# Output rows in transfers of 64 instead of 32, the last ones shared anew among three queues

## The chip, the cores and the metric

The kernel runs on one core of a Trainium2 chip. That core has TensorE (PE, matrix products into PSUM), VectorE (DVE), ScalarE (ACT), GpSimd (POOL) and the sync engine (SP), which only issues. DMA transfers are issued by SP, ScalarE and GpSimd, each on a queue of its own, and carried by 16 DMA engines that all queues use. The metric is the device time of one execution in microseconds (us).

## The reference

Two layers, one behind the other, with B = 8 batches, H = 8 heads, S = 576 time steps, D = 64, and H x D = 512 channels.

```python
kv  = einsum('bhsd,bhse->bhde', k, v)
o   = einsum('bhsd,bhde->bhse', q, kv)
x   = o / sqrt(mean(o*o, axis=-1) + 1e-6) * g_norm    # heads side by side: (8, 576, 512)
proj = x @ w_proj                                     # (8, 576, 1536): x1, x2, x3
conv = irfft(rfft(x2, axis=1) * rfft(filter, axis=0)) # circular, over time
out  = (x1 * conv * x3) @ w_out                       # (8, 576, 512) float32
```

The output is 8 x 576 rows of 512 float32 numbers, 2048 bytes a row and 9.44 MB in all.

## The kernel before

Everything is computed with the channels on the partitions and time along the free dimension, up to the last product, which turns this round: it takes 128 time steps as the output's partitions and 512 channels as its free dimension. The time steps lie on chip in a permuted order, in blocks of 32: one block holds steps that are 6 apart in time (`t_of`, line 156). So 32 neighbouring partitions of an output tile are 32 rows of the result that lie 6 x 2048 bytes apart.

The order of the work is written out by hand. `ORDER` (line 20) is a list of steps, `name.batch`, and the last loop (line 871) calls them one after the other; each engine and each queue executes its instructions in the order in which they were issued. The schedule interleaves up to four batches: loads (`Lk`, `Lv`, `Lq`: on the GpSimd queue, float32 in HBM, bf16 on chip, `load` at line 161), `K` (k times v), `Qt` (a DMA transpose of q on the sync queue, line 433), `O` (q times kv), the norm, the gates `Ga`/`Gb`, the forward transform `F`, products with the filter's transform `M`, the inverse `I`, `u`/`w`/`fin`, and the output product.

The output is made by these steps:

- `U0.b` and `U2.b`: each two products of 128 rows for batch b into one pair of PSUM banks. `ot0.b` and `ot2.b` copy them with ScalarE into a tile `ot` of 128 x 2 x 512 float32 (line 822) and issue its transfers through `o_dma` (line 789).
- `U4.b` for odd b: the 64 rows left over of batch b-1 and the 64 left over of batch b, as one product of 128 rows; `ot4` copies it (line 835).
- `V0.7` to `V3.7`: the last 512 rows of batch 7 (its U0 and U2 are replaced by these four). The copies `vv`, `va` (line 859; V3 is copied in two halves of the columns, one by VectorE and one by ScalarE) and each transfer have steps of their own; `ds`, `dg`, `da` issue on SP, GpSimd, ScalarE, and `da31` is column block 3, piece 1 of a tile, on ScalarE.

The tiles of `ot` come from three buffers in turn for the first 15 uses; the last five use the space of tiles that are no longer needed (`sq`, `o`, `rstd`, `x` of batch 6 and `x2`; line 806). A buffer is written again when its transfers have landed.

`out_qs` (line 796) chooses the queues: SP for the batches 0 to 5; for 6 and 7 SP and GpSimd in turn, and for their `ot4` ScalarE too. In all, 144 transfers of 32 rows (64 KB): 124 on SP, 14 on GpSimd, 6 on ScalarE.

One more transfer matters for the prediction: line 260 loads the 64 numbers of `g_norm` twice, side by side, into `g_row`, with a source pattern of [[0, 1], [0, 2], [1, 64]] (step and count of each dimension, the outermost first).

Of the kernel before, what the change touches and what calls it, by code (L numbers as in the profile page):

```python
# [19 lines left out]
ORDER = """Lf.0 Zi.0 Z.0 W.3.2 Zt.0 An.0 W.0.12 Act.0 Zg.0 Gc.0 W.1.3 Zd.0 Zf.0 Tb1.0 Lvb.0 Lkb.0 Zz.0 Ff2.0 Ff1.0 Tb0.0 Lqb.0  # L20
Ff0.0 Kb.0 eKb.0 T1.0 eTv1.0 Tb2.0 Lqa.0 T0.0 eTv0.0 O23.0 Lka.0 W.2.2 sq2.0 ov2.0 Lva.0 sq3.0 ov3.0 R3.0 rs3.0 R2.0
Lv.1 Ka.0 Lk.1 eKa.0 Lq.1 rs2.0 x1.0 Zc.0 H0.0 O01.0 sq1.0 sq0.0 ov1.0 H1.0 Lw1.0 ov0.0 R1.0 rs1.0 H2.0 W.4.2 K.1 eK.1
T1.1 eTa1.1 R0.0 rs0.0 x0.0 Lw3.0 fd0.0 HN1.0 fa0.0 HN0.0 T0.1 O23.1 sq3.1 ob3.1 eTa0.1 Ga1.0 fd1.0 Ga0.0 sq2.1 ob2.1
Lw2.0 x11.0 x10.0 O01.1 sq0.1 fa1.0 ob0.1 fr0.0 Gb0.0 g0.0 Gb1.0 Lq.2 g1.0 Ga2.0 fr1.0 sq1.1 ob1.1 x12.0 R0.1 rs0.1
Lk.2 abT.0 eT.0 R3.1 R2.1 rs3.1 rs2.1 x1.1 Lv.2 rrM.0 rrT.0 R1.1 rs1.1 err.0 abM.0 eab.0 T0.2 F0.0 Lk.3 eTs0.2 x0.1
fd.1 fr.1 T1.2 eTs1.2 Ga3.0 x13.0 K.2 eK.2 M0.0 Gb3.0 g3.0 F2.0 O01.2 sq0.2 ob0.2 Lv.3 sq1.2 F2t.0 M2.0 Gb2.0 g2.0
F1.0 F1t.0 ob1.2 O23.2 sq2.2 ob2.2 M1.0 Av1.0 rrM.1 rrT.1 err.1 Ga1.1 x11.1 Gb1.1 Ga3.1 Lk.4 sq3.2 F0.1 ob3.2 g1.1
x13.1 R2.2 rs2.2 R0.2 rs0.2 fa.1 abT.1 eT.1 Gb3.1 A0.0 M0.1 R1.2 g3.1 R3.2 rs3.2 x1.2 rs1.2 x0.2 fd.2 Lv.4 K.4 eK.4
Lq.3 abM.1 eab.1 I23.0 es23.0 K.3 eK.3 Io01.0 Ga0.1 fr.2 os01.0 Gb0.1 x10.1 Io23.0 I01.0 Ga2.1 Lq.4 os23.0 fa.2 A0.1
es01.0 g0.1 x12.1 F2.1 F2t.1 M2.1 Qt.3 O23.3 Gb2.1 g2.1 sq2.3 ob2.3 sq3.3 ob3.3 Qt.4 Ga0.2 x10.2 F1.1 O01.3 sq0.3  # L30
ob0.3 F1t.1 u.0 sq1.3 ob1.3 M1.1 abM.2 eab.2 Ga1.2 x11.2 R0.3 rs0.3 rrM.2 w.0 Av1.1 R1.3 rs1.3 rrT.2 R3.3 err.2 Qh.3
Gb1.2 rs3.3 R2.3 rs2.3 Lk.6 fin.0 g1.2 Lv.5 abT.2 eT.2 I01.1 es01.1 Io01.1 os01.1 x1.3 x0.3 fd.3 Ga3.2 x13.2 O23.4
sq3.4 ob3.4 fa.3 Gb0.2 g0.2 Gb3.2 sq2.4 ob2.4 F0.2 g3.2 Lk.5 I23.1 es23.1 Io23.1 os23.1 Ga2.2 F1.2 F1t.2 x12.2 M0.2
O01.4 abM.3 sq0.4 ob0.4 Qh.4 M1.2 sq1.4 ob1.4 F2.2 eab.3 F2t.2 Lwo.0 Lv.6 Lq.6 M2.2 Gb2.2 g2.2 Lq.5 R0.4 rs0.4 R2.4
rs2.4 Qt.5 K.5 R1.4 rs1.4 U0.0 A0.2 Av1.2 Io23.2 eK.5 ot0.0 u.1 os23.2 abT.3 eT.3 w.1 R3.4 Io01.2 os01.2 I01.2 es01.2
Ga0.3 x10.3 K.6 Gb0.3 fr.3 rrM.3 rs3.4 rrT.3 eK.6 Ga1.3 err.3 F1.3 fin.1 g0.3 Qt.6 x11.3 F1t.3 x0.4 O01.5 sq0.5 ob0.5
sq1.5 ob1.5 x1.4 fd.4 M1.3 U2.0 ot2.0 Gb1.3 fa.4 I23.2 g1.3 fr.4 es23.2 Ga2.3 x12.3 O23.5 sq3.5 sq2.5 ob2.5 ob3.5 F0.3
M0.3 U0.1 ot0.1 Ga3.3 x13.3 F2.3 A0.3 F2t.3 R0.5 R1.5 rs1.5 M2.3 Gb3.3 g3.3 R3.5 rs3.5 Gb2.3 rs0.5 g2.3 x0.5 R2.5
rs2.5 x1.5 abT.4 eT.4 Av1.3 Lv.7 O01.6 sq0.6 sq1.6 fd.5 ob0.6 ob1.6 Lk.7 U4.1 ot4.1 abM.4 u.2 eab.4 R1.6 rs1.6 Io23.3
rrM.4 rrT.4 os23.3 err.4 I01.3 es01.3 fr.5 Ga1.4 x11.4 Lq.7 I23.3 Io01.3 os01.3 Ga0.4 es23.3 x10.4 Gb0.4 w.2 fin.2  # L40
Qh.5 g0.4 R0.6 rs0.6 Ga2.4 x12.4 O23.6 sq3.6 ob3.6 Qt.7 u.3 sq2.6 ob2.6 F0.4 M0.4 rrM.5 rrT.5 err.5 Gb1.4 g1.4 F1.4
F2.4 F2t.4 M2.4 F1t.4 R3.6 rs3.6 A0.4 Gb2.4 R2.6 g2.4 Ga3.4 x13.4 rs2.6 Ga0.5 x10.5 K.7 eK.7 M1.4 Av1.4 U2.2 ot2.2
fa.5 I23.4 es23.4 Qh.6 Gb3.4 g3.4 x0.6 Io01.4 os01.4 x1.6 fr.6 abT.5 eT.5 O01.7 sq1.7 ob1.7 w.3 U2.1 sq0.7 ot2.1 ob0.7
Ga1.5 x11.5 fd.6 I01.4 es01.4 abM.5 eab.5 R0.7 rs0.7 fin.3 Io23.4 os23.4 fa.6 Gb1.5 F0.5 g1.5 M0.5 A0.5 F2.5 F2t.5
M2.5 rrM.6 rrT.6 err.6 U0.2 ot0.2 Gb0.5 F1.5 g0.5 O23.7 sq2.7 sq3.7 F1t.5 Qh.7 ob3.7 M1.5 U2.3 ob2.7 ot2.3 Ga3.5 x13.5
R2.7 rs2.7 Av1.5 u.4 w.4 fin.4 R3.7 U4.3 ot4.3 rs3.7 Gb3.5 I01.5 es01.5 I23.5 es23.5 Ga1.6 Io23.5 os23.5 g3.5 abM.6
eab.6 x11.6 F0.6 Ga2.5 abT.6 x12.5 M0.6 F1.6 Gb2.5 eT.6 Io01.5 g2.5 os01.5 F2.6 F2t.6 M2.6 F1t.6 M1.6 U0.3 Av1.6 ot0.3
u.5 U0.4 ot0.4 R1.7 rs1.7 x0.7 Ga0.6 x10.6 A0.6 Io01.6 os01.6 I01.6 es01.6 Gb1.6 g1.6 Io23.6 os23.6 I23.6 es23.6 U2.4
Gb0.6 x1.7 GaP.7 fd.7 fr.7 rrM.7 ot2.4 fa.7 rrT.7 err.7 abM.7 x1P.7 eab.7 abT.7 g0.6 F0.7 F1.7 w.5 eT.7 F2.7 F2t.7
fin.5 F1t.7 M0.7 A0.7 M2.7 U0.5 ot0.5 M1.7 U2.5 Ga2.6 ot2.5 Av1.7 u.6 Gb2.6 Gb3.6 Ga3.6 x12.6 g2.6 J01.7 x13.6 g3.6  # L50
Jo01.7 os01.7 w.6 fin.6 J23.7 Jo23.7 os23.7 es23.7 u23.7 Ga1.7 x11.7 es01.7 u01.7 Gb0.7 Ga0.7 x10.7 U0.6 ot0.6 Gb1.7
U2.6 g1.7 g0.7 fu01.7 ot2.6 GbP.7 U4.5 ot4.5 gP.7 fin23P.7 U4.7 ot4.7 V0.7 vv0.7 da02.7 ds00.7 dg01.7 GaQ.7 x1Q.7
ds03.7 GbQ.7 gQ.7 fin23Q.7 V1.7 va1.7 da12.7 ds10.7 dg13.7 dg11.7 V2.7 vv2.7 ds23.7 da22.7 dg21.7 V3.7 vv3q.7 va3p.7
ds20.7 ds30.7 da31.7 ds32.7 da33.7"""


@with_exitstack
def kernel(
# [332 lines left out]
    for n_, (d_, s_) in dict(Lw1=(wp[:, :, 0:DM], moe_w_proj[:, 0:DM]), Lw2=(wp[:, :, DM:2 * DM], moe_w_proj[:, DM:2 * DM]),  # L391
                             Lw3=(wp[:, :, 2 * DM:D3], moe_w_proj[:, 2 * DM:D3]), Lwo=(wo, moe_w_out)).items():
# [393 lines left out]
    step["u"] = lambda b: inv_u(b, 0, NDC)  # L786


    def o_dma(b, blk, t, qs, pieces=range(4)):
        for i in pieces:  # L790
            g, r = blk + i // 2, i % 2
            row = b * S + SB * (g // 3) + 2 * (g % 3) + r
            qs[i % len(qs)].dma_start(out=bass.AP(tensor=out.tensor, offset=out.offset + row * DM, ap=[[6 * DM, 32], [1, DM]]),
                                      in_=t[32 * i:32 * i + 32])
# [25 lines left out]
    def U_ev(b, c0):  # L820
        ot = ot_tile(b, c0)
        act.copy(out=ot, in_=tmp['u', b, c0])  # L822
# [10 lines left out]
    def U4_ev(b):  # L833
        ot = ot_tile(b, 4)
        act.copy(out=ot[:, 0], in_=tmp['u4', b])
        free(("u4", b))
        o_dma(b - 1, 8, ot[:, 0], out_qs(b, 4))
# [10 lines left out]
    def V(b, c):  # L848
        for h in range(1 if c < 3 else 2):
            n = DM if c < 3 else DM // 2  # L850
            t = take(("v", c, h), 1 + (c + h) % 2)
            tmp['v', c, h] = t[:, 0] if (c + h) % 2 else t
            for dc in range(NDC):
                mm2(tmp['v', c, h][:, 0:n], ygt(b)[:, dc, 64 + c * P:64 + (c + 1) * P], wo[:, dc, h * n:(h + 1) * n],
                                 start=(dc == 0), stop=(dc == NDC - 1))

    def V_ev(b, c, h, ev):
        n = DM if c < 3 else DM // 2
        ev(out=ot_tile(b, c // 2 * 2)[:, c % 2, h * n:(h + 1) * n], in_=tmp['v', c, h][:, 0:n])
# [47 lines left out]
```

## Time and profile before

| | |
|---|---|
| median of 3 runs | 214.08 us (214.07 to 215.18) |
| the profiled execution | 215.22 us, its span 213.4 us, mean TensorE clock 0.987 |
| TensorE busy | 201.6 us, 94% of the span |
| ScalarE, VectorE, GpSimd busy | 154.8, 174.8, 58.6 us |
| bytes moved by DMA | 29.61 MB; HBM read 33.69 MB, written 9.44 MB |
| output transfers on SP from `ot` | 108 of 64 KB, 1.7 us from issue to landing (median) |

The span runs from the first to the last instruction of the profiled execution; its time is measured around it. Issues of transfers appear in the profile under the queue that issues them (SPq, ACTq, or POOL), with the time that the issue took; the time to landing is from the start of the issue to the last completion. Packets are the single pieces that the DMA engines move; each transfer adds small packets of 4 bytes that report its completion.

### The profile page before, as it was taken

To read this page: it belongs to the slowest core of one execution; us is meant where nothing else is said; L and a number is where in the kernel's file an instruction comes from. 1 tells how busy PE (TensorE), PEld (TensorE's weight loads), DVE (VectorE), ACT (ScalarE), POOL (GpSimd) and SP (SyncE) were. 2 spreads that over 40 slices of the span, in tenths; PEclk is the share of its full clock that TensorE was granted. 3 is DMA by queue.
4 is the path that set the end of the run, shared out by engine and by line. 5 is a ranking of instruction groups with operands and counts; after the bars stand their busy time and mean duration, and the time that the engine had idled before them with its cause. 6 is when DMAs were issued, how large, how long until landed. Compare 5 with 4: busy or idle time off the path is not lost.

```text
span 213.4 us, 5926 instructions
## 1 busy us (share of the span) xinstructions
PE 201.6 (94%) x2472; PEld 135.3 (63%) x2472; DVE 174.8 (82%) x242; ACT 154.8 (73%) x249; POOL 58.6 (27%) x86
## 2 busy tenths in 40 slices
PE   7998779999998999999999999999999999999991
PEld 5564447576786677677665868675575574476550
DVE  6565887599893999999979999899896999997631
ACT  3787786999787998897989985794866565345430
POOL 7970391027007800400053004002201200400642
PEclk9999988999999999999999999999999999999997
DMA  4999999999999999955749944151450254051475
GB/s 64 181 203 202 205 178 200 204 197 158 197 141 182 158 205 204 196 97 117 154 114 138 235 81 96 28 136 40 98 136 16 49 139 109 20 142 41 118 214 160
DMA packets 39966, 29.61 MB, mean 139 GB/s; under 512 B 14500, under 2 KB 35556, under 8 KB 39940
## 3 DMA queue, kind: packets, MB, share of 16 engines
q0 software_dynamic: 22016, 17.76, 54.0%
q1 hardware_dynamic: 17636, 11.08, 23.1%
q10 hardware_dynamic: 288, 0.39, 0.6%
q8 instruction: 19, 0.31, 0.6%
q14 instruction: 7, 0.06, 0.1%
HBM read 33.69 MB, written 9.44 MB: 202 GB/s over the span
## 4 chain that ended last, share of the span: by engine, by line
PE 72%; DMA 12%; DVE 5%; POOL 4%; ACT 2%; issue 2%; POOLq 0%; DVEq 0%; ACTq 0%
PE ps L112 32%; PE ps L115 32%; DMA vb<-in_v_dram 9%; DMA qT<-qb 3%; PE ps L485 2%; PE ps L408 2%; PE ps L574 1%; POOL Y L652 1%; DVE tpw L646 1%; PE ps L638 1%; ACT rstd L512 1%; PE ps L612 1%; DVE x L526 1%; DVE HM L380 1%; PE ps L632 1%
## 5 line engine op out<-in xcount | busy, mean ns | idle before, releaser
L652 POOL TENSOR_TENSOR Y<-tpw 97x1024 bf16<-97x1024 f32 x8 | 18.9, 2360 | 108.9 <-DVE tpw L646 69.7
L112 PE MATMUL ps<-x,wp 128*128 128x288 bf16 (+2 forms) x264 | 37.8, 295 | 0.9 <-DVE x L526 0.7
L646 DVE TENSOR_TENSOR tpw<-ps,HH 97x2048 f32<-97x2048 f32 (+1 forms) x16 | 36.6, 2288 | 1.7 <-PE ps L112 0.9
L115 PE MATMUL ps<-x,wp 128*64 128x288 bf16 x496 | 34.6, 286 | 0.0
L112 PEld LDWEIGHTS <-wp 128*128 128x128 bf16 x264 | 26.0, 100 | 10.7 <-issue 1.9
L679 DVE TENSOR_TENSOR g<-ps,x 128x576 bf16<-128x576 f32 x30 | 22.5, 756 | 10.7 <-PE ps L112 5.3
L115 PEld LDWEIGHTS <-wp 128*64 128x64 bf16 x496 | 28.0, 110 | 3.5 <-issue 0.7
L591 ACT CAST x<-ps 128x1024 bf16<-128x1024 f32 (+1 forms) x24 | 21.0, 879 | 8.4 <-PE ps L574 5.6
L512 ACT ACTIVATE rstd<-ps,bias_eps 128x576 bf16<-128x576 f32 x32 | 23.0, 748 | 5.3 <-PE ps L115 2.5
L677 ACT CAST x<-ps 128x576 bf16<-128x576 f32 x30 | 19.6, 652 | 7.9 <-PE ps L112 4.6
L112 PE MATMUL ps<-wo,yg 128*128 128x512 bf16 (+1 forms) x104 | 23.6, 372 | 0.2 <-DVE yg L767 0.2
L739 ACT CAST eo<-ps 128x576 bf16<-128x576 f32 x32 | 19.9, 659 | 5.1 <-PE ps L112 3.8
L501 ACT ACTIVATE sq<-ps 128x576 bf16<-128x576 f32 x32 | 20.4, 653 | 3.1 <-PE ps L485 3.1
L508 ACT ACTIVATE o<-ps,g_col 128x576 bf16<-128x576 f32 x28 | 20.6, 748 | 0.0
L822 ACT COPY ot<-ps 128x1024 f32<-128x1024 f32 x12 | 12.2, 1016 | 8.9 <-PE ps L112 7.6
L115 PE MATMUL ps<-wp,ab 128*64 128x512 bf16 x144 | 17.5, 380 | 0.0
L112 PEld LDWEIGHTS <-yg 128*128 128x128 bf16 x104 | 9.6, 98 | 11.6 <-issue 1.4
L526 DVE TENSOR_TENSOR x<-o,rstd 128x1152 bf16<-128x1152 bf16 x16 | 11.6, 753 | 4.8 <-ACT rstd L512 4.8
L115 PEld LDWEIGHTS <-ind 128*64 128x64 bf16 x130 | 9.8, 121 | 7.2 <-DVE HH L380 1.8
L661 DVE TENSOR_TENSOR Y<-ps,HM 128x1024 bf16<-128x1024 f32 x8 | 9.8, 1223 | 3.2 <-PE ps L638 3.1
L115 PEld LDWEIGHTS <-ab 128*64 128x64 bf16 x144 | 7.9, 110 | 5.9 <-issue 0.3
L115 PE MATMUL ps<-wo,yg 128*64 128x512 bf16 x88 | 10.6, 380 | 0.0
(159 smaller groups left out, 347.0 us busy)
## 6 DMA issues: line engine op xcount, KB each, us to landing
out_dram<-ot SPq DMA_DIRECT2D x108, 64.0 KB, 1.7
vb<-in_v_dram POOLq DMA_DIRECT2D x7, 576.0 KB, 11.3
kb<-in_k_dram POOLq DMA_DIRECT2D x7, 576.0 KB, 11.1
qb<-in_q_dram POOLq DMA_DIRECT2D x7, 576.0 KB, 13.2
wp<-in_moe_w_proj_dram POOLq DMA_DIRECT2D x3, 512.0 KB, 15.2
fn<-in_moe_filter_fft_dram POOLq DMA_DIRECT2D x1, 576.0 KB, 6.5
vb<-in_v_dram POOLq DMA_DIRECT2D x2, 288.0 KB, 7.3
kb<-in_k_dram POOLq DMA_DIRECT2D x2, 288.0 KB, 6.8
```

The source lines that it names most:

```text
L112: nc.tensor.matmul(out, lhsT, rhs, start=start, stop=stop)
L115: nc.tensor.matmul(out[c:min(c + 64, m)], lhsT[:, c:min(c + 64, m)], rhs, start=start, stop=stop, tile_position=(0, c))
L501: act.activation(out=halves(sq()[:, j]), in_=tmp['o', b, j][:, :, 0:TH], func=AF.Square)
L508: act.activation(out=by_time(osb(), j), in_=i_, func=AF.Copy, scale=g_col)
L512: act.activation(out=by_time(rstd(), j), in_=by_row(tmp['r', b, j]), func=AF.Abs_reciprocal_sqrt, scale=1.0 / D, bias=bias_eps)
L526: vec.tensor_mul(out=xt(b)[:, j0:j1], in0=osb()[:, j0:j1], in1=rstd()[:, j0:j1])
L591: act.copy(out=o_(), in_=tmp[key, b])
L646: vec.tensor_mul(out=t_[:n], in0=xp[:n].unsqueeze(1).to_broadcast([n, 2, 2, DM]), in1=two)
L652: op(out=Yt()[:n, 2 * g:2 * g + 2], in0=t_[:n, ::-1, 0], in1=t_[:n, ::-1, 1])
L677: act.copy(out=x1, in_=pp[:, :, 0:TH])
L679: vec.tensor_mul(out=halves(g13t(b)[:, dc]), in0=pp[:, :, 0:TH], in1=x1)
L739: act.copy(out=eo()[:, h, d0:d0 + 2], in_=tmp['i', b, d0, h][:, :, 0:TH])
```

## The change

`o_dma` issues two transfers per tile of 128 rows in place of four. Each takes 64 neighbouring partitions, which are two blocks of 32: the DRAM side has a new outermost dimension of 2 with a step of one row (the two row phases of a group), and inside it the 32 rows that are 6 rows apart. `out_qs` no longer gives ScalarE a share of `ot4.7`. The transfers of V0 to V3 are 8 in place of 16, on SP (4), GpSimd (2) and ScalarE (2). In all there are 72 transfers of 128 KB: 63 on SP, 7 on GpSimd, 2 on ScalarE. `ORDER` is broken into lines elsewhere; beside this only its last steps differ.

```diff
...
-Jo01.7 ... V0.7 vv0.7 da02.7 ds00.7 dg01.7 GaQ.7 x1Q.7
-ds03.7 GbQ.7 gQ.7 fin23Q.7 V1.7 va1.7 da12.7 ds10.7 dg13.7 dg11.7 V2.7 vv2.7 ds23.7 da22.7 dg21.7 V3.7 vv3q.7 va3p.7
-ds20.7 ds30.7 da31.7 ds32.7 da33.7"""
+Jo01.7 ... V0.7
+vv0.7 ds00.7 dg01.7 GaQ.7 x1Q.7 GbQ.7 gQ.7 fin23Q.7 V1.7 va1.7 ds10.7 da11.7 V2.7 vv2.7 dg20.7 ds21.7
+V3.7 vv3q.7 va3p.7 da30.7 ds31.7"""
...
-    def o_dma(b, blk, t, qs, pieces=range(4)):
+    def o_dma(b, blk, t, qs, pieces=range(2)):
         for i in pieces:
-            g, r = blk + i // 2, i % 2
-            row = b * S + SB * (g // 3) + 2 * (g % 3) + r
-            qs[i % len(qs)].dma_start(out=bass.AP(tensor=out.tensor, offset=out.offset + row * DM, ap=[[6 * DM, 32], [1, DM]]),
-                                      in_=t[32 * i:32 * i + 32])
+            g = blk + i
+            row = b * S + SB * (g // 3) + 2 * (g % 3)
+            qs[i % len(qs)].dma_start(out=bass.AP(tensor=out.tensor, offset=out.offset + row * DM, ap=[[DM, 2], [6 * DM, 32], [1, DM]]),
+                                      in_=t[64 * i:64 * i + 64])
 
     def out_qs(b, c):
-        if b < B - 2:
-            return (nc.sync,)
-        return (nc.sync, nc.gpsimd) if c < 4 else (nc.sync, nc.gpsimd, nc.scalar, nc.gpsimd)
+        return (nc.sync,) if b < B - 2 else (nc.sync, nc.gpsimd)
...
-        for i in range(4):
+        for i in range(2):
             for e, q_ in (("s", nc.sync), ("g", nc.gpsimd), ("a", nc.scalar)):
                 step["d%s%d%d" % (e, c, i)] = lambda b, c=c, i=i, q_=q_: o_dma(b, 1 + 2 * c, ot_tile(b, c // 2 * 2)[:, c % 2], (q_,), (i,))
```

More of the change, by code (lines that the diff above doesn't have):

```diff
@@ L17 @@
 MAGIC = 3.0 * (2.0 ** 22)
[L20 to L52, printed above, removed]
-ds03.7 GbQ.7 gQ.7 fin23Q.7 V1.7 va1.7 da12.7 ds10.7 dg13.7 dg11.7 V2.7 vv2.7 ds23.7 da22.7 dg21.7 V3.7 vv3q.7 va3p.7
@@ L54 @@
-ds20.7 ds30.7 da31.7 ds32.7 da33.7"""
+ORDER = """Lf.0 Zi.0 Z.0 W.3.2 Zt.0 An.0 W.0.12 Act.0 Zg.0 Gc.0 W.1.3 Zd.0 Zf.0 Tb1.0 Lvb.0 Lkb.0
+Zz.0 Ff2.0 Ff1.0 Tb0.0 Lqb.0 Ff0.0 Kb.0 eKb.0 T1.0 eTv1.0 Tb2.0 Lqa.0 T0.0 eTv0.0 O23.0 Lka.0
+W.2.2 sq2.0 ov2.0 Lva.0 sq3.0 ov3.0 R3.0 rs3.0 R2.0 Lv.1 Ka.0 Lk.1 eKa.0 Lq.1 rs2.0 x1.0
+Zc.0 H0.0 O01.0 sq1.0 sq0.0 ov1.0 H1.0 Lw1.0 ov0.0 R1.0 rs1.0 H2.0 W.4.2 K.1 eK.1 T1.1
+eTa1.1 R0.0 rs0.0 x0.0 Lw3.0 fd0.0 HN1.0 fa0.0 HN0.0 T0.1 O23.1 sq3.1 ob3.1 eTa0.1 Ga1.0 fd1.0
@@ new lines @@
+Ga0.0 sq2.1 ob2.1 Lw2.0 x11.0 x10.0 O01.1 sq0.1 fa1.0 ob0.1 fr0.0 Gb0.0 g0.0 Gb1.0 Lq.2 g1.0
+Ga2.0 fr1.0 sq1.1 ob1.1 x12.0 R0.1 rs0.1 Lk.2 abT.0 eT.0 R3.1 R2.1 rs3.1 rs2.1 x1.1 Lv.2
+rrM.0 rrT.0 R1.1 rs1.1 err.0 abM.0 eab.0 T0.2 F0.0 Lk.3 eTs0.2 x0.1 fd.1 fr.1 T1.2 eTs1.2
+Ga3.0 x13.0 K.2 eK.2 M0.0 Gb3.0 g3.0 F2.0 O01.2 sq0.2 ob0.2 Lv.3 sq1.2 F2t.0 M2.0 Gb2.0
+g2.0 F1.0 F1t.0 ob1.2 O23.2 sq2.2 ob2.2 M1.0 Av1.0 rrM.1 rrT.1 err.1 Ga1.1 x11.1 Gb1.1 Ga3.1
+Lk.4 sq3.2 F0.1 ob3.2 g1.1 x13.1 R2.2 rs2.2 R0.2 rs0.2 fa.1 abT.1 eT.1 Gb3.1 A0.0 M0.1
@@ new lines @@
+R1.2 g3.1 R3.2 rs3.2 x1.2 rs1.2 x0.2 fd.2 Lv.4 K.4 eK.4 Lq.3 abM.1 eab.1 I23.0 es23.0
+K.3 eK.3 Io01.0 Ga0.1 fr.2 os01.0 Gb0.1 x10.1 Io23.0 I01.0 Ga2.1 Lq.4 os23.0 fa.2 A0.1 es01.0
+g0.1 x12.1 F2.1 F2t.1 M2.1 Qt.3 O23.3 Gb2.1 g2.1 sq2.3 ob2.3 sq3.3 ob3.3 Qt.4 Ga0.2 x10.2
+F1.1 O01.3 sq0.3 ob0.3 F1t.1 u.0 sq1.3 ob1.3 M1.1 abM.2 eab.2 Ga1.2 x11.2 R0.3 rs0.3 rrM.2
+w.0 Av1.1 R1.3 rs1.3 rrT.2 R3.3 err.2 Qh.3 Gb1.2 rs3.3 R2.3 rs2.3 Lk.6 fin.0 g1.2 Lv.5
+abT.2 eT.2 I01.1 es01.1 Io01.1 os01.1 x1.3 x0.3 fd.3 Ga3.2 x13.2 O23.4 sq3.4 ob3.4 fa.3 Gb0.2
@@ new lines @@
+g0.2 Gb3.2 sq2.4 ob2.4 F0.2 g3.2 Lk.5 I23.1 es23.1 Io23.1 os23.1 Ga2.2 F1.2 F1t.2 x12.2 M0.2
+O01.4 abM.3 sq0.4 ob0.4 Qh.4 M1.2 sq1.4 ob1.4 F2.2 eab.3 F2t.2 Lwo.0 Lv.6 Lq.6 M2.2 Gb2.2
+g2.2 Lq.5 R0.4 rs0.4 R2.4 rs2.4 Qt.5 K.5 R1.4 rs1.4 U0.0 A0.2 Av1.2 Io23.2 eK.5 ot0.0
+u.1 os23.2 abT.3 eT.3 w.1 R3.4 Io01.2 os01.2 I01.2 es01.2 Ga0.3 x10.3 K.6 Gb0.3 fr.3 rrM.3
+rs3.4 rrT.3 eK.6 Ga1.3 err.3 F1.3 fin.1 g0.3 Qt.6 x11.3 F1t.3 x0.4 O01.5 sq0.5 ob0.5 sq1.5
+ob1.5 x1.4 fd.4 M1.3 U2.0 ot2.0 Gb1.3 fa.4 I23.2 g1.3 fr.4 es23.2 Ga2.3 x12.3 O23.5 sq3.5
@@ new lines @@
+sq2.5 ob2.5 ob3.5 F0.3 M0.3 U0.1 ot0.1 Ga3.3 x13.3 F2.3 A0.3 F2t.3 R0.5 R1.5 rs1.5 M2.3
+Gb3.3 g3.3 R3.5 rs3.5 Gb2.3 rs0.5 g2.3 x0.5 R2.5 rs2.5 x1.5 abT.4 eT.4 Av1.3 Lv.7 O01.6
+sq0.6 sq1.6 fd.5 ob0.6 ob1.6 Lk.7 U4.1 ot4.1 abM.4 u.2 eab.4 R1.6 rs1.6 Io23.3 rrM.4 rrT.4
+os23.3 err.4 I01.3 es01.3 fr.5 Ga1.4 x11.4 Lq.7 I23.3 Io01.3 os01.3 Ga0.4 es23.3 x10.4 Gb0.4 w.2
+fin.2 Qh.5 g0.4 R0.6 rs0.6 Ga2.4 x12.4 O23.6 sq3.6 ob3.6 Qt.7 u.3 sq2.6 ob2.6 F0.4 M0.4
+rrM.5 rrT.5 err.5 Gb1.4 g1.4 F1.4 F2.4 F2t.4 M2.4 F1t.4 R3.6 rs3.6 A0.4 Gb2.4 R2.6 g2.4
@@ new lines @@
+Ga3.4 x13.4 rs2.6 Ga0.5 x10.5 K.7 eK.7 M1.4 Av1.4 U2.2 ot2.2 fa.5 I23.4 es23.4 Qh.6 Gb3.4
+g3.4 x0.6 Io01.4 os01.4 x1.6 fr.6 abT.5 eT.5 O01.7 sq1.7 ob1.7 w.3 U2.1 sq0.7 ot2.1 ob0.7
+Ga1.5 x11.5 fd.6 I01.4 es01.4 abM.5 eab.5 R0.7 rs0.7 fin.3 Io23.4 os23.4 fa.6 Gb1.5 F0.5 g1.5
+M0.5 A0.5 F2.5 F2t.5 M2.5 rrM.6 rrT.6 err.6 U0.2 ot0.2 Gb0.5 F1.5 g0.5 O23.7 sq2.7 sq3.7
+F1t.5 Qh.7 ob3.7 M1.5 U2.3 ob2.7 ot2.3 Ga3.5 x13.5 R2.7 rs2.7 Av1.5 u.4 w.4 fin.4 R3.7
+U4.3 ot4.3 rs3.7 Gb3.5 I01.5 es01.5 I23.5 es23.5 Ga1.6 Io23.5 os23.5 g3.5 abM.6 eab.6 x11.6 F0.6
@@ new lines @@
+Ga2.5 abT.6 x12.5 M0.6 F1.6 Gb2.5 eT.6 Io01.5 g2.5 os01.5 F2.6 F2t.6 M2.6 F1t.6 M1.6 U0.3
+Av1.6 ot0.3 u.5 U0.4 ot0.4 R1.7 rs1.7 x0.7 Ga0.6 x10.6 A0.6 Io01.6 os01.6 I01.6 es01.6 Gb1.6
+g1.6 Io23.6 os23.6 I23.6 es23.6 U2.4 Gb0.6 x1.7 GaP.7 fd.7 fr.7 rrM.7 ot2.4 fa.7 rrT.7 err.7
+abM.7 x1P.7 eab.7 abT.7 g0.6 F0.7 F1.7 w.5 eT.7 F2.7 F2t.7 fin.5 F1t.7 M0.7 A0.7 M2.7
+U0.5 ot0.5 M1.7 U2.5 Ga2.6 ot2.5 Av1.7 u.6 Gb2.6 Gb3.6 Ga3.6 x12.6 g2.6 J01.7 x13.6 g3.6
+Jo01.7 os01.7 w.6 fin.6 J23.7 Jo23.7 os23.7 es23.7 u23.7 Ga1.7 x11.7 es01.7 u01.7 Gb0.7 Ga0.7 x10.7
@@ L57 @@
+U0.6 ot0.6 Gb1.7 U2.6 g1.7 g0.7 fu01.7 ot2.6 GbP.7 U4.5 ot4.5 gP.7 fin23P.7 U4.7 ot4.7 V0.7
+vv0.7 ds00.7 dg01.7 GaQ.7 x1Q.7 GbQ.7 gQ.7 fin23Q.7 V1.7 va1.7 ds10.7 da11.7 V2.7 vv2.7 dg20.7 ds21.7
+V3.7 vv3q.7 va3p.7 da30.7 ds31.7"""
 @with_exitstack
```

## The prediction

> **What bounds the kernel now.** I read the engine table and the chain of waits first, then the issues and queues of the DMA engines, because the change touches nothing but output transfers.
>
> ```profile
> PE 201.6 (94%) x2472; PEld 135.3 (63%) x2472; DVE 174.8 (82%) x242; ACT 154.8 (73%) x249; POOL 58.6 (27%) x86
> ...
> PE 72%; DMA 12%; DVE 5%; POOL 4%; ACT 2%; issue 2%; POOLq 0%; DVEq 0%; ACTq 0%
> ```
>
> TensorE bounds it: 94% of the span, 72% of the chain that ended last. Output transfers appear in that chain only in its last microseconds. The second place to look is the sync queue's own timeline (start, duration, queue, line, operation, count), because it gives the moments at which output appears:
>
> ```profile
> 95.97 4.78 SPq L793 DMA_DIRECT2D out_dram<-ot  x8
> 100.91 2.88 SPq L433 DMA_TRANSPOSE qT<-qb  x1
> 104.62 14.34 SPq L793 DMA_DIRECT2D out_dram<-ot  x20
> 126.27 2.92 SPq L433 DMA_TRANSPOSE qT<-qb  x1
> 135.97 56.74 SPq L793 DMA_DIRECT2D out_dram<-ot  x76
> 198.58 1.72 SPq L793 DMA_DIRECT2D out_dram<-sq  x4
> 201.29 1.82 SPq L793 DMA_DIRECT2D out_dram<-o  x4
> ```
>
> Nothing leaves before 95.97 us. The rest of the sync queue's share is 4 transfers from `ot` (the program's U4.5), 1 from `rstd` and 7 from `x` after 203 us. Third, the queues and the issues, which tell how one transfer is spread over the 16 DMA engines:
>
> ```profile
> DMA packets 39966, 29.61 MB, mean 139 GB/s; under 512 B 14500, under 2 KB 35556, under 8 KB 39940
> ## 3 DMA queue, kind: packets, MB, share of 16 engines
> q0 software_dynamic: 22016, 17.76, 54.0%
> q1 hardware_dynamic: 17636, 11.08, 23.1%
> q10 hardware_dynamic: 288, 0.39, 0.6%
> ...
> HBM read 33.69 MB, written 9.44 MB: 202 GB/s over the span
> ```
>
> ```profile
> out_dram<-ot SPq DMA_DIRECT2D x108, 64.0 KB, 1.7
> ...
> out_dram<-x SPq DMA_DIRECT2D x7, 64.0 KB, 1.8
> out_dram<-x ACTq DMA_DIRECT2D x5, 64.0 KB, 1.8
> ...
> qT<-qb SPq DMA_TRANSPOSE x5, 4.9
> out_dram<-rstd ACTq DMA_DIRECT2D x1, 64.0 KB, 2.2
> ...
> g_row<-in_g_norm_dram SPq DMA_DIRECT2D x1, 0.5 KB
> ```
>
> **How a transfer is shared out.** Queue 10 is ScalarE's: 5 + 1 transfers of 32 rows are 192 packets of 2 KB, and it counts 288, so each transfer adds 16 small packets: one completion for each of 16 engines. Its access pattern has 32 as outermost count on both sides. Now the sync queue, whose 17636 packets hold one transfer of another kind. Its 124 output transfers make 124 x 48 = 5952. The 11684 left are five transposes and the load of `g_row`. A transpose of 576 KB in pieces of 256 B (the size of the packets recorded at that queue beside the 2 KB rows) is 2304, and with 32 completions 2336; five make 11680. That leaves 4 for `g_row`: two pieces of 256 B and two completions. Line 260 describes `g_row` with an outermost count of 2 (behind a count of 1), and it ran on two engines. So the rows show 16 shares where the outermost count is 32 and two where it is 2.
>
> The changed `o_dma` describes the DRAM side as [[DM, 2], [6*DM, 32], [1, DM]]: the outermost count is 2, not 32; the SBUF side counts 64 partitions. If the outermost count decides, 128 KB go through two engines and fourteen stand idle. That is the step on which the forecast rests, and it is inferred from one small transfer.
>
> The Trainium skill, "DMA: Bandwidth & Descriptors", on why a DMA increments its semaphore by 16, states it as a rule: the number of engines is the largest up to 16 that divides the size of the slowest dimension, other than 1, on both sides. The packets of `g_row` agree with it. The same section says that the sync and scalar queues then take the lowest-numbered engines; no view here names an engine.
>
> **The change part by part.** *Transfers.* 144 transfers of 32 rows become 72 of 64. By the code, batches 0 to 5 issue all on the sync queue, the two last share: sync 63 (4 + 10 + 38 + 2 + 2 + 2 + 1 + 4 in the order of the timeline above), ScalarE 2, GpSimd 7.
>
> *Price of a row on an engine.* What an engine can carry is read where the DMA engines are full, in the windows (PE, PEld, DVE, ACT, POOL, clock, DMA share, GB/s):
>
> ```profile
> 20.00:40.00 20.00, 17.06 (x226) 11.17 (x226) 14.33 (x28) 16.04 (x27) 7.54 (x8) 0.91 1.26 196
> ...
> 150.00:160.00 10.00, 10.00 (x83) 6.38 (x80) 9.57 (x10) 7.54 (x12) 0.79 (x2) 1.00 0.49 122
> ```
>
> The loads of 20 to 40 us are counted in the bf16 that they write (q0's 17.76 MB, 0.92 MB of it output, against 33.69 MB read from HBM), so 196 GB/s written are 392 GB/s read, 24.5 GB/s for each engine. A row of 2048 B then takes 84 ns. The other end is queue 10: 0.6% of 16 x 213.4 us is 20.5 us for 192 rows, 107 ns with all that two rows on one engine cost each other. (From 150 to 160 us, 122 GB/s at a share of 0.49 give 132 ns, but there two packets overlap on an engine and both are counted.) I take 84 ns, since two engines with a standing backlog are full as in the load stretch; the single packets of queue 10 mostly took 84, and none under 81.
>
> *Price of the output.* A transfer of 64 rows on two engines is 32 rows each: 32 x 84 ns = 2.69 us, where 32 rows on sixteen took two row times. If it is the same two engines each time, the 65 transfers of sync and ScalarE need 65 x 2.69 = 174.7 us on that pair. The trace has no room for that: from 95.97 to 213.4 us are 117.4 us.
>
> *What else the pair carries.* Three whole loads start at 111 to 113 us:
>
> ```profile
> L163 POOL DMA_DIRECT2D vb<-in_v_dram x9: 669/780/1102, 4.4 to 111.4; - x9
> L163 POOL DMA_DIRECT2D kb<-in_k_dram x9: 669/769/792, 5.5 to 112.2; - x9
> L163 POOL DMA_DIRECT2D qb<-in_q_dram x9: 679/769/797, 6.2 to 113.0; - x9
> ```
>
> Each reads 1.18 MB, 1/16 of it on each engine: 3.0 us at 24.5 GB/s, 9.0 for the three. The transposes of 100.91 and 126.27 us have their shares there too; I take their issue time of 2.9 us each (nothing at the least, 4.9 at the most, their time to landing), 5.8 in all.
>
> *Is the pair ever idle?* The first 4 transfers keep it busy to about 108; the 10 from 104.62 on, with loads and a transpose, to about 146; the next come at 136. The 38 from there on need 102 us, and they appeared within 57. ScalarE then stalls, for the evacuation at line 822 or 835 waits until its `ot` buffer, the third last used, is empty:
>
> ```profile
> ACT ot L822 <- PE ps L112: 7.6, 5, 3.1
> ...
> 155.12 0.58 ACT L835 COPY ot<-ps 128x512 f32<-128x512 f32 x1
> 167.13 1.01 ACT L822 COPY ot<-ps 128x1024 f32<-128x1024 f32 x1 [2.08 <-PE ps L112]
> ```
>
> Now it waits for TensorE only. Behind it on ScalarE stand the squares, roots and evacuations of the next batch, and TensorE waits for their PSUM. But when a buffer comes free two others are still queued, 16 us of work at the least, and the longest gap between evacuations is the 12.0 us above: production catches up each time, the pair does not idle. The transpose of 126.27 stands on the pair behind 14 output transfers and would land near 149; TensorE reads it here,
>
> ```profile
> 137.58 0.37 PE ps L485 x8
> ```
>
> so a stall of ten microseconds goes there, while the pair still has work.
>
> *Issue time.* The durations of the sync queue's issues (shortest, median, longest):
>
> ```profile
> L793 SPq DMA_DIRECT2D out_dram<-ot x108: 314/424/1619, 96.0 to 204.6; - x108
> ```
>
> An issue of 32 rows takes 424 ns; I put 64 rows between 314 (the shortest) and 848 (twice). Even 63 x 0.85 = 54 us lie beside the pair's 175. The regrouped order at the end saves issues, but these queue behind the pair.
>
> *Other bounds.* A completion could hold an engine between transfers. Issues 0.42 us apart put 0.17 us of data on each engine and still land after 1.7 us, so it is 0.25 at the most: 65 x 0.25 = 16 us more. I take nothing.
>
> *Sum.* 95.97 (first issue) + 1.7 (its way to landing) + 174.7 + 9.0 + 5.8 + 0.9 = 288.1 us of span. The 0.9 is from the last landing to the end: the last issue and its row,
>
> ```profile
> 210.75 0.46 SPq L793 DMA_DIRECT2D out_dram<-x  x1
> ```
>
> with 1.8 to landing is 212.5, and the span ends at 213.4. That is 74.7 above the span before. The profiled execution took 215.22 us, 1.8 around its span and 1.1 above the median (its granted clock fell to 0.91 early); on the median, 214.08 + 74.7 = **289 us**.
>
> With 107 ns a row the sum is 337; with 81 ns, and the pair's other work slipping in beside the rows, 268. The Trainium skill, "DMA: Bandwidth & Descriptors", Specifications, gives about 27 GiB/s for an engine; by that a row is 71 ns and the estimate 261, but no stretch of this trace shows an engine that fast.
>
> **The rivals.** *Sixteen shares after all: faster.* If the 64 partitions decide, or the pattern reaches the hardware in another form, each engine gets four rows. Then only the end counts. The last evacuations are done at 209.45; before, the sync queue issued until 211.21:
>
> ```profile
> 209.08 0.37 ACT L859 COPY x<-ps 128x256 f32<-128x256 f32 x1 [1.56 <-PE ps L112]
> 209.48 0.79 ACTq L793 DMA_DIRECT2D out_dram<-x  x2
> ```
>
> After, both pieces of V3 are issued at 209.5 on two queues and land 1.8 to 2.1 later, at about 211.5: 1.0 us earlier, 213.1 us, and 212.4 to 214.1 with an issue of 314 to 848 ns and a landing of 1.6 to 2.3. For it: the SBUF side has 64. Against it: `g_row`.
>
> *Two engines, but others each time.* Then no pair fills up, but each transfer needs 30 row times more, 2.5 us; the last, issued at 209.5, lands at 213.8, 1.3 us after the one before: 215.4 us. No row speaks for or against, except that nothing in these instructions names an engine, so that a turning choice needs a state of its own.
>
> *The pair, with half the price.* If an engine overlapped its rows so that they cost 42 ns, the pair would need 87 us, less than the 117 there are, and only the last tiles would queue: about 217 us. The full engines of 20 to 40 us speak against it; I count it with the case before.
>
> **How the numbers follow.** One fixed pair 0.84; pairs in turn or a faster pair 0.04; sixteen shares 0.12. What a measurement of this kernel can tell from no change is about 0.5%, 1.1 us. The sixteen shares lie around that bound: 0.07 faster, 0.05 the same. Slower is 0.88. The range is the fixed pair's: 265 (268, less most of the 1.7 and 0.9 at the two ends, which may be covered) to 337 (107 ns a row). It leaves out 0.16 for the others, and some 0.04 of its own.
>
> **What would show it.** Right: the sync queue counts about 63 x (64 + 2) packets of output in place of 63 x (64 + 16); landing of an output transfer grows from 1.7 to many microseconds; waits of `ot` evacuations on output DMA appear at lines 822 and 835; the mean DMA share stays low after 136 us at about 50 GB/s while TensorE has gaps; the chain of waits is DMA from there to the end. Wrong: landing near 2 us with a span near 213 (sixteen shares); landing near 4.2 us with TensorE as full as before (pairs in turn); a pair that idles between 100 and 136 us, or rows well above 107 ns, would put it outside the range.

## The result and the profile after

The changed kernel takes 291.91 us (median of 6 runs, 290.41 to 294.72); the kernel before took 214.07 us beside it. The ratio is 1.365, 95% interval 1.357 to 1.373. The forecast was 289 us with a range of 265 to 337. Medians here are over all executions; ratios leave out executions that lie more than 1.5% above the fastest of the same kernel.

These are lines from the profile page of the changed kernel: its engine table, three of its rows over time (40 slices; busy shares in tenths, and GB/s moved), two of its queues (packets, MB, share of 16 engines) and the shares of the chain of work that ended last:

```profile
span 290.3 us, 5835 instructions
...
PE 209.8 (72%) x2472; PEld 139.9 (48%) x2472; DVE 175.3 (60%) x242; ACT 155.0 (53%) x249; POOL 55.9 (19%) x79
...
PE   8987999999999979999149999405994299800000
...
DMA  6999999999996937911931111111111111521110
GB/s 91 199 203 207 181 203 203 202 151 180 205 204 119 53 100 123 169 38 44 68 89 48 54 51 54 51 51 51 54 51 51 51 54 55 131 63 48 51 51 30
...
q1 hardware_dynamic: 15842, 11.21, 20.0%
...
q10 hardware_dynamic: 132, 0.26, 0.2%
...
DMA 37%; PE 25%; DVE 10%; SPq 7%; ACT 4%; issue 3%; POOL 2%; ACTq 0%; POOLq 0%; DVEq 0%
```

TensorE does the same work (209.8 us against 201.6) in 77 us more. From the middle on it has holes, and in the last five slices it does nothing. The share of the DMA engines sinks to one tenth there, mostly at 51 to 55 GB/s. In the chain that ended last DMA has 37%, where it had 12%, and TensorE 25% in place of 72%.

The packets tell why. 63 sync transfers of 64 rows with two completions each are 63 x 66 = 4158 packets; the five transposes and `g_row` are 11684 as before; together they are 15842, the number of queue 1. For queue 10, 2 x 66 = 132. So each output transfer of the sync queue and of ScalarE's queue ran on two engines.

Where the backlog holds, the windows (PE, PEld, DVE, ACT, POOL, clock, DMA share, GB/s) show what two engines carry:

```profile
170.00:190.00 20.00, 14.82 (x109) 9.15 (x107) 13.24 (x13) 6.94 (x11) 2.35 (x1) 0.94 0.13 52
190.00:210.00 20.00, 10.15 (x60) 6.44 (x61) 8.17 (x14) 5.65 (x9) 0.00 (x0) 0.63 0.13 52
...
270.00:273.00 3.00, 0.00 (x0) 0.00 (x0) 0.00 (x0) 0.00 (x0) 0.00 (x0) 0.50 0.13 51
```

The share of 0.13 is two of sixteen, and 51 GB/s are 25.5 for each engine: 80 ns for a row of 2048 B. Several transfers are under way at any time (issues of 169.59, 195.10 and 215.62 us land 13.4 to 13.6 us later), so if they had used different pairs, more than two engines would have been busy: it is the same pair each time. The last row lies where transfers of ScalarE's queue are under way beside the sync queue's (its second is issued at 268.88 us): the sum stays at 51, so both queues use the same two engines.

The waits (who waited for whom, us in total, times, longest):

```profile
POOL Y L661 <- DVE tpw L655: 104.3, 4, 34.8
ACT ot L829 <- DMA out_dram<-ot: 48.0, 7, 14.4
...
PE ps L121 <- ACT ot L829: 24.2, 3, 14.7
```

The second and third row are new: ScalarE waits 48 us, in seven stalls, for an `ot` buffer to empty, and TensorE waits behind it for PSUM. (GpSimd's wait in the first row was 69.7 us before; it has time.) The sync queue's timeline has the 8, 20 and 76 transfers of before as 4, 10 and 38:

```profile
93.12 2.77 SPq L802 DMA_DIRECT2D out_dram<-ot  x4
96.06 11.52 SPq L442 DMA_TRANSPOSE qT<-qb  x1
107.62 29.34 SPq L802 DMA_DIRECT2D out_dram<-ot  x10
137.79 10.34 SPq L442 DMA_TRANSPOSE qT<-qb  x1
148.23 90.78 SPq L802 DMA_DIRECT2D out_dram<-ot  x38
242.88 2.19 SPq L802 DMA_DIRECT2D out_dram<-sq  x2
```

The `sq` tile, which left at 198.58 us, leaves at 242.88: 44 us of the loss lie before that point, where ScalarE's seven stalls are. The other 33 come after it, while the last tiles drain: from `sq` to the end are 47 us in place of 15.

### The profile page after: what moved, and what is told of

Read it like the earlier page. It is cut to its first block, busy times and chain, and to the rows that moved or that the text cites. A ratio compares the mean times of both kernels' runs of the same rounds, so it can differ in the third digit from the quotient of the medians.

```text
span 290.3 us, 5835 instructions
## 1 busy us (share of the span) xinstructions
PE 209.8 (72%) x2472; PEld 139.9 (48%) x2472; DVE 175.3 (60%) x242; ACT 155.0 (53%) x249; POOL 55.9 (19%) x79
## 3 DMA queue, kind: packets, MB, share of 16 engines
q1 hardware_dynamic: 15842, 11.21, 20.0%
## 4 chain that ended last, share of the span: by engine, by line
DMA 37%; PE 25%; DVE 10%; SPq 7%; ACT 4%; issue 3%; POOL 2%; ACTq 0%; POOLq 0%; DVEq 0%
DMA out_dram<-ot 14%; PE ps L124 13%; DMA qb<-in_q_dram 10%; SPq L802 7%; PE ps L121 7%; DMA out_dram<-sq 5%; DMA vb<-in_v_dram 5%; DMA qT<-qb 4%; DVE tpw L655 2%; ACT ot L829 1%; PE ps L417 1%; PE ps L362 1%; DVE HH L389 1%; DVE Y L670 1%; PE ps L494 1%
## 5 line engine op out<-in xcount | busy, mean ns | idle before, releaser
L121 PE MATMUL ps<-x,wp 128*128 128x288 bf16 (+2 forms) x264 | 39.8, 302 | 10.4 <-ACT ot L829 9.5
L121 PEld LDWEIGHTS <-wp 128*128 128x128 bf16 x264 | 26.6, 102 | 21.4 <-issue 11.9
L124 PE MATMUL ps<-wp,ab 128*64 128x512 bf16 x144 | 18.4, 394 | 7.0 <-ACT ot L829 7.0
L121 PE MATMUL ps<-IV,Y 128*128 128x192 bf16 (+3 forms) x90 | 11.6, 288 | 14.7 <-ACT ot L829 14.7
L121 PEld LDWEIGHTS <-Y 128*128 128x128 bf16 (+1 forms) x90 | 8.9, 113 | 17.3 <-issue 14.8
L560 DVE TENSOR_TENSOR ab<-d__539 128x768 bf16<-128x768 bf16 (+1 forms) x18 | 8.5, 508 | 11.8 <-PE ps L124 11.7
L124 PEld LDWEIGHTS <-ab 128*64 128x64 bf16 x144 | 8.6, 112 | 13.0 <-DVE d__539 L546 6.8
```

The costliest lines, as they stand in the source:

```text
L121: nc.tensor.matmul(out, lhsT, rhs, start=start, stop=stop)
L124: nc.tensor.matmul(out[c:min(c + 64, m)], lhsT[:, c:min(c + 64, m)], rhs, start=start, stop=stop, tile_position=(0, c))
```

## The experiments

Theory A: the outermost count of the access pattern decides how many DMA engines carry a transfer; 2 confines it to two, the same two each time. Theory B: a transfer of 64 rows is costly by itself. Theory C: the new shares of the queues at the end cost something of their own. The kernel before was timed again beside each run, on the same chip.

### The two outer dimensions exchanged

```diff
-            qs[i % len(qs)].dma_start(... ap=[[DM, 2], [6 * DM, 32], [1, DM]]),
+            qs[i % len(qs)].dma_start(... ap=[[6 * DM, 32], [DM, 2], [1, DM]]),
...
```

> The changed kernel with the two outer dimensions of the DRAM side exchanged: [[6*DM, 32], [DM, 2], [1, DM]] in place of [[DM, 2], [6*DM, 32], [1, DM]]. Size, count, queues and order of the transfers and the set of addresses stay; the rows of a group of 64 come out in another order, so the output is not the reference's. Theory A (the outermost count of 2 confines a transfer to two engines): 32 is now outermost, all sixteen engines carry it, the time falls back to 212.5 to 215 us, each sync transfer has 16 completions and lands in about 2 us. Theory B (64 rows in one transfer are costly by themselves, in descriptors or in issue): still 280 us or more.

Measured: 212.88 us (211.94 to 214.44) against 213.86, ratio 0.996 (0.9928 to 0.9993). These are its queues, the row of its output transfers (KB each, us to landing) and the durations of their issues (ns, shortest, median, longest):

```profile
q1 hardware_dynamic: 16724, 11.21, 25.4%
q10 hardware_dynamic: 160, 0.26, 0.3%
...
out_dram<-ot SPq DMA_DIRECT2D x54, 128.0 KB, 2.4
```

```profile
L802 SPq DMA_DIRECT2D out_dram<-ot x54: 533/596/1976, 94.6 to 201.0; - x54
```

63 x (64 + 16) + 11684 = 16724: sixteen completions. A transfer of 128 KB lands after 2.4 us, and its issue takes 0.60 us. Nothing but the order of two dimensions was changed (so that the rows of a group come out in another order), and the whole loss is gone. A holds, B falls.

### The new shares of the queues alone

```diff
             g = blk + i
-            row = b * S + SB * (g // 3) + 2 * (g % 3)
-            qs[i % len(qs)].dma_start(... ap=[[DM, 2], [6 * DM, 32], [1, DM]]), in_=t[64 * i:64 * i + 64])
+            for r in range(2):
+                row = b * S + SB * (g // 3) + 2 * (g % 3) + r
+                qs[i % len(qs)].dma_start(... ap=[[6 * DM, 32], [1, DM]]), in_=t[64 * i + 32 * r:64 * i + 32 * r + 32])
```

> The changed kernel's order and its shares of the queues, but every transfer of 64 rows issued as two of 32 rows, one behind the other on the same queue, with the access pattern of before. Theory A: nothing of the loss is left, 213.5 to 216 us (the last transfers may queue a little longer: sync and ScalarE issue two each behind V3). Theory C (the new shares of the queues at the end cost something of their own): more than 217 us.

Measured: 214.64 us against 213.86, ratio 1.0038 (1.001 to 1.0067). By the medians 0.8 us belongs to the shares, by the upper end of the interval 1.4 us; C falls as an explanation of a loss of 78 us.

### 64 rows joined in another direction

The two column blocks of one `ot` tile leave together, 32 partitions at a time; every row goes where it went before.

```diff
+    def o_dma_two(b, blk, t, qs, pieces=range(4)):
+        row = lambda g: SB * (g // 3) + 2 * (g % 3)
+        for i in pieces:
+            g, r = blk + i // 2, i % 2
+            qs[i % len(qs)].dma_start(out=bass.AP(tensor=out.tensor, offset=out.offset + (b * S + row(g) + r) * DM,
+                                                  ap=[[6 * DM, 32], [(row(g + 2) - row(g)) * DM, 2], [1, DM]]),
+                                      in_=t[32 * i:32 * i + 32])
...
-        for i in range(2):
-            o_dma(b, b % 2 + 2 * (c0 + i), ot[:, i], out_qs(b, c0))
+        o_dma_two(b, b % 2 + 2 * c0, ot, out_qs(b, c0))
```

> The kernel before, with the 64 rows joined in another direction: 32 partitions and both column blocks of an ot tile, outermost count 32 on both sides, for U0 and U2 of all batches; U4 and the last four blocks as before. Output as the reference's. Theory A: the same time as before, 213 to 215 us, since a transfer of 128 KB on sixteen engines costs no more than two of 64 KB and the sync queue bounds nothing. Theory B: as slow as the changed kernel, or at least 240 us.

Measured: 213.13 us against 213.86, ratio 0.9978 (0.9946 to 1.001). Its queue 1 counts 16804 packets: 52 x (64 + 16) + 20 x (32 + 16) + 11684, so its transfers of 64 rows ran on sixteen engines. It was timed again, with 12 executions:

> The kernel with two column blocks in one transfer once more, timed in more rounds: whether its 0.9978 (0.9946 to 1.001) is a gain. If 64 rows per transfer on sixteen engines save something at the end: 0.996 to 0.999 with the interval below 1. If not: an interval that holds 1.

Measured: 213.82 us against 213.54, ratio 1.0041 (1.0005 to 1.0078). That is neither of the two outcomes expected: the interval lies just above 1. The two ratios lie on both sides of 1, 0.6% apart. So 64 rows per transfer on sixteen engines neither cost nor save anything that can be shown, and the 0.4% of the exchanged dimensions, measured once, cannot be taken for a gain either.

A last step to a faster kernel let V2 and V3 leave together as well (on top of the kernel above):

```diff
-ds03.7 ... V2.7 vv2.7 ds23.7 da22.7 dg21.7 V3.7 vv3q.7 va3p.7
-ds20.7 ds30.7 da31.7 ds32.7 da33.7"""
+ds03.7 ... V2.7 vv2.7 V3.7 vv3q.7 va3p.7
+ps20.7 pa21.7 ps22.7 pa23.7"""
...
+                step["p%s%d%d" % (e, c, i)] = ... o_dma_two(b, 1 + 2 * c, ot_tile(b, c), (q_,), (i,))
```

> As the kernel with two column blocks in one transfer, and also V2 and V3 leave together, in four transfers of 32 partitions and two column blocks behind V3's copies, two on the sync queue and two on ScalarE's, in place of eight on three queues. Theory A, and the end of the kernel before bounded by the sync queue's last issues (to 211.2 us of the span): last issue at about 209.9 us, end 0.3 to 0.9 us earlier, 213.2 to 213.8 us. If instead the 512 KB that now leave at once bound the end: 214 to 215 us.

Measured: 213.84 us against 213.86, ratio 1.0005 (0.9975 to 1.0035). That lies between the two expectations. From ScalarE's last copy of V3 to the end its trace has 5.6 us (206.08 to 211.7), the kernel before 4.3 (209.08 to 213.4). The saving of issues may be paid for by the 512 KB that leave at once; no run isolates that. No version here is shown to beat the kernel before.

### The change in the last two batches alone, and in the others alone

Two functions, `o_dma32` (as before) and the changed one; the first kernel uses the old one for batches 0 to 5, the second for 6, 7 and the last blocks.

```diff
-            o_dma(b, b % 2 + 2 * (c0 + i), ot[:, i], out_qs(b, c0))
+            (o_dma32 if b < B - 2 else o_dma)(b, b % 2 + 2 * (c0 + i), ot[:, i], out_qs(b, c0))
```

The issue of `U4` is changed in the same way, and the second kernel swaps the two functions.

> The change in the last two batches alone: batches 0 to 5 leave in transfers of 32 rows as before, batches 6 and 7 and the last blocks as in the changed kernel. Theory A with one fixed pair: the pair gets 9 sync and 2 ScalarE transfers (11 x 32 rows at the 80 ns that the changed kernel's plateau shows: 28 us) from 198.6 us on, so the span ends at 228 to 232 us, time about 230 us. If the pair changes from transfer to transfer: about 216 us.

> The change in batches 0 to 5 alone: 54 sync transfers of 64 rows with outermost count 2; batches 6 and 7 and the last blocks in transfers of 32 rows as before. Theory A with one fixed pair: the 11 transfers of the end no longer stand on the pair, 11 x 32 x 80 ns = 28 us less than the changed kernel, less what the 32-row transfers still need there (1/16 of it), 262 to 268 us. If only the end were at fault: 214 us.

Measured: 240.23 us for the end alone, 266.19 for the other batches alone, against 213.88. The two losses, 26.4 and 52.3 us, add up to 78.7; the whole change lost 77.8. The second came out as expected. The first was expected near 230: a pair that changes from transfer to transfer (216) is excluded, but 10 us were not in the account. Two of its windows:

```profile
200.00:205.00 5.00, 4.78 (x31) 2.73 (x30) 2.48 (x4) 2.24 (x4) 1.98 (x3) 1.00 0.31 37
...
225.00:230.00 5.00, 0.00 (x0) 0.00 (x0) 0.00 (x0) 0.00 (x0) 0.00 (x0) 0.50 0.13 51
```

From 200 to 205 us the DMA engines move 37 GB/s in all, less than the 51 of the plateau, although GpSimd's queue carries transfers beside the pair (a share of 0.31 is five busy engines). The packet records of this trace tell how much the pair lost. From 200 to 216 us, while GpSimd's transfers were under way, the sync queue started 343 rows of 2048 B; 128 of them are the four transfers of 32 rows of U4.5, which use all engines. The 215 left are the pair's, where its plateau of 25 rows per us would have given 398. That is 7 of the 10 us. I suspected GpSimd's transfers, which have an outermost count of 2 too, and gave those 32 rows each:

```diff
+            if qs[i % len(qs)] is nc.gpsimd:
+                o_dma32(b, blk, t, (nc.gpsimd,), (2 * i, 2 * i + 1))
+                continue
```

> The kernel with the change in the last two batches alone, and there GpSimd's seven transfers of 64 rows issued as fourteen of 32 rows (outermost count 32), so that only the 9 sync and 2 ScalarE transfers run on two engines. If GpSimd's two-engine transfers are what slows the pair at the end (its rows came at half the plateau's pace while they were under way): the 28 us of the pair from 200 us on remain, span 229 to 231 us, time 230 to 233 us. If GpSimd has no part in it: as with them, 238 us or more.

Measured: 234.58 and 238.15 us against 213.54. By the rule given with the result only the first counts; the second is the one that was traced. 234.58 lies between the two expectations, 5.6 us below the 240.23 of the kernel without this edit, but one execution does not settle that difference. In the trace, the pair carried 254 rows from 200 to 216 us in place of 215, which is 1.6 us more work done, and still far from 398. As far as this trace shows, then, GpSimd's two-engine transfers are only a small part of the shortfall. GpSimd's 32-row transfers, which use all sixteen engines, landed after 6.2 to 7.4 us (medians by tile) in place of 2.0 to 2.3; two of their sixteen shares stand on the full pair. Why the pair falls short of its plateau while other queues' transfers run on its engines stays open.

### An outermost count of 4

```diff
+    def o_dma128(b, blk, t, qs):
+        if blk % 3 == 2 or blk == 8:
+            o_dma(b, blk, t, qs)
+            return
+        row = b * S + SB * (blk // 3) + 2 * (blk % 3)
+        qs[0].dma_start(out=bass.AP(... ap=[[DM, 4], [6 * DM, 32], [1, DM]]), in_=t)
...
-            o_dma(b, b % 2 + 2 * (c0 + i), ot[:, i], out_qs(b, c0))
+            (o_dma128 if b < B - 2 else o_dma)(b, b % 2 + 2 * (c0 + i), ot[:, i], out_qs(b, c0))
```

> The kernel before, with batches 0 to 5 in transfers of 128 rows and outermost count 4, [[DM, 4], [6*DM, 32], [1, DM]], for three of four tiles (where the two groups of 64 rows adjoin; the fourth and U4 as two of 64 rows with outermost count 2). Theory A: a transfer of 128 rows runs on four engines, so it takes 32 row times as one of 64 rows did; its completions are 4. Two of the four engines carry both kinds: 18 x 32 + 12 x 32 + 6 x 32 rows = 1152 rows x 80 ns = 92 us in about 100 us: close to full but little backlog, 216 to 235 us. If the count of engines did not follow the outermost count but the size or the queue: 285 us and more.

Measured: 216.4 us (215.92 and 216.87) against 213.88, ratio 1.014 (1.004 to 1.024), so some loss is likely but its size is unclear. The kernel differs from the words of its expectation in one point: the tiles whose groups don't adjoin, and U4, went out as four transfers of 32 rows, so that the four engines had only 18 x 32 = 576 rows each of that kind, 46 us at 80 ns a row. The expected 216 to 235 us were worked out for more work than that, and the time by itself confirms little. Its queue does:

```profile
q1 hardware_dynamic: 16556, 11.08, 24.3%
```

18 x (128 + 4) + 52 x (32 + 16) + 11684 = 16556: four completions for an outermost count of 4. With 2, 4 and 32 outermost the counts are 2, 4 and 16. ScalarE's waits for `ot` buffers are 6.2 us in place of 48.0:

```profile
ACT ot L829 <- DMA out_dram<-ot: 6.2, 2, 5.0
```

### Batches 0 to 5 on GpSimd's queue

```diff
-        return (nc.sync,) if b < B - 2 else (nc.sync, nc.gpsimd)
+        return (nc.gpsimd,) if b < B - 2 else (nc.sync, nc.gpsimd)
```

> The changed kernel with batches 0 to 5 on GpSimd's queue in place of the sync queue; outermost count 2 stays. If every transfer with outermost count 2 goes to the same two engines, whatever the queue: 280 us or more. If GpSimd's queue takes other engines from transfer to transfer: no pair fills up, 215 to 235 us (its issues of 0.67 us stand before the additions of line 661 on GpSimd, 54 x 0.67 = 36 us more on an engine that was busy for 59).

Measured: 254.88 us against 213.88. Both ranges of the expectation were missed, for they forgot that the end, on the sync queue's pair, costs its 26 us here too. What is left are 15 us before it: `sq` is copied at 212.32 us in place of 197.55. Whether GpSimd's transfers also share one pair is told by a window in which its queue alone moves data:

```profile
150.00:170.00 20.00, 20.00 (x176) 12.41 (x171) 17.43 (x17) 13.67 (x21) 9.07 (x12) 1.00 0.41 90
```

90 GB/s at a share of 0.41 is more than two engines carry, and TensorE is full; so GpSimd's output is not held to one pair. Its transfers landed after 7.7 us there (median), where the same 64 rows landed after 2.6 to 2.7 us from GpSimd's queue with the exchanged dimensions. That fits few engines for each transfer and other ones from one to the next, but no view names the engines. The Trainium skill, "DMA: Bandwidth & Descriptors", on why a DMA increments its semaphore by 16, says the same of both queues: the lowest-numbered engines for SP and ScalarE, consecutive ones from a cursor that moves on for GpSimd. The 15 us fit the waits that GpSimd's in-order queue now has before the additions of line 661, but that was not isolated:

```profile
POOL out_dram L802 <- ACT ot L829: 46.7, 8, 9.1
```

## Why the prediction was right

**Two engines.** The step on which all rested, inferred from the four packets of `g_row`, held: 15842 and 132 packets, and the exchanged dimensions undo the loss. The Trainium skill, "DMA: Bandwidth & Descriptors", Rules for kernel authors, warns that an outermost dimension of size c below 16 confines a DMA to at most c engines; the outermost counts 2, 4 and 32 here, with 2, 4 and 16 completions, agree.

**One fixed pair.** The forecast gave it 0.84 without a row that names an engine. The plateau at 51 to 52 GB/s and a share of 0.13 to 0.14, from 160 to 240 us, settles it for the sync queue, and ScalarE's queue shares it.

**The price of a row.** Forecast 84 ns from the full engines of 20 to 40 us; the plateau shows 80. At 51 GB/s a transfer of 128 KB takes 2.57 us, and the 65 transfers 167 us in place of 174.7.

**The sum.** The first issue came at 93.1 us in place of 96.0; the path and the end (1.7 and 0.9) are kept; 290.3 - 93.1 - 1.7 - 0.9 - 167 leaves 27.6 us of other work on the pair, where 14.8 were forecast. That is the mis-sized term: errors of -2.9 and -7.7 were made good by one of +12.8, so that the forecast came this close is in part luck. Its parts can be told by counting: up to 148.23 us the pair had 14 transfers, 36 us of rows in 55, so 19 us of loads, transposes and gaps (two of 1.8 us by the packet records); from there 51 transfers are 131 us of rows in about 140, so some 9 us are lost. About half of them lie from 243 to 262 us, where GpSimd's seven transfers run: the pair's queues started 359 rows there, where the plateau would have given 473, which is 4.6 us. These transfers the forecast had priced at nothing on the pair; the end alone shows a surplus of the same kind.

**Never idle.** Right but for the two gaps, which begin at 107.0 and 147.7 us: each time the sync queue was still issuing a transpose (until 107.6 and 148.1) while the pair ran dry. That the issue of a transpose would take ten microseconds was not in the forecast. Production stalled at line 829 and caught up each time. One reading was wrong: the longest gap between evacuations of the kernel before is not 12.0 us but 18.3, from 116.6 to 134.9 us. It did no harm, for the pair did not run dry in that stretch.

**The stall at the transpose.** The forecast sent ten microseconds of TensorE's wait there. It was 4.3 for the transposed q; the wait of 6.7 at 137.4 us was already one for ScalarE and its buffer. The total did not depend on it.

**The issue time.** This step was wrong. For 64 rows I put 0.31 to 0.85 us; the durations in the changed kernel are

```profile
L802 SPq DMA_DIRECT2D out_dram<-ot x54: 511/2440/4829, 93.1 to 257.3; - x54
```

a median of 2.44, about the 2.57 that the pair takes for a transfer. On sixteen engines the same 64 rows took 0.60, so this is not work of the issuer: it is held up by the full pair. A wait for an earlier transfer's landing is not the reason: the sync queue's waits at line 802 name no output transfer, and the 13.4 to 13.6 us from the start of an issue to its landing are 5.3 transfers of the pair, fewer than the eight that the program allows to be open (see the last section). As far as the rows show it entered the sum by the two gaps alone, since the pair sets the end.

**The rivals.** Sixteen shares is what the exchanged dimensions gave, at 212.9 us where 213.1 was worked out. Engines that change from transfer to transfer fit what GpSimd's queue shows; on the sync queue they are excluded.

## What to carry to other kernels

When transfers are joined, look at the outermost dimension of both access patterns before looking at the bytes: joining along a dimension of 2 took fourteen of sixteen engines away and cost 36%, joining 64 rows along a dimension of 32 cost nothing that the runs show. The number of completion packets of a queue (here 66 or 80 for a transfer of 64 rows) tells the share from any profile, and one small odd transfer in the profile of before can show the rule in advance. And where the queue that would be relieved bounds nothing, there was nothing to win: the Trainium skill's advice to coalesce many small transfers ("DMA: Bandwidth & Descriptors", Rules for kernel authors), which names 64 KB as the bound, brought no gain that these runs show at 128 KB against 64 KB.

## What the runs showed of the hardware that was not expected

A full pair holds up the issuing queue, and everything behind it. Beside the 2.44 us of an output issue, two DMA transposes took 11.52 and 10.34 us to issue on the sync queue where they took 2.9 before. In the end-alone kernel four transfers of 32 rows behind the backlog took 9.28 us to issue, where they took 1.81 before:

```profile
202.99 9.28 SPq L802 DMA_DIRECT2D out_dram<-ot  x4
```

GpSimd's transfers of 64 rows landed after 9.1 to 10.1 us (medians by tile) in the changed kernel, but how much of this the full pair adds is not shown: without a backlog they took 7.7 us in the window above. Clearer is the run in which GpSimd's transfers had 32 rows on sixteen engines, 6.2 to 7.4 us in place of 2.0 to 2.3.

A transfer of SP or ScalarE also waits until the one eight before has landed. The program gives these transfers eight semaphores in turn, and each issue waits for the value that the last transfer on its semaphore leaves. ScalarE's transfer of V1 shares a semaphore with the first `sq` transfer of the sync queue, with which it has nothing else in common, and the copy of V3 stands behind it on ScalarE. The chain of waits shows it:

```profile
242.88 14.32 DMA out_dram<-sq
257.23 0.04 issue
257.27 1.14 ACTq L802
258.41 0.04 issue
258.45 0.37 ACT x L866
```

The copy of V3 waited 6.6 us. In the kernel before, ScalarE waited for no landing, and the sync queue's longest wait for one at an output issue was 1.3 us.
